# Attention and mixing with the last 64 rows, tokens and keys padded to 128

## Chip, cores and metric

One core of a Trainium2 chip. The metric is the device time of one execution in microseconds. Three runs of the kernel before took 1993.06, 1989.41 and 1990.96 us, a median of 1990.96.

## What is computed

Three stages follow each other on 8 batches (B) of 576 tokens (S) and 512 channels, all float32:

```
k_p, v_p = mean of k, v over groups of 8 keys          (576 -> 72 keys, 8 heads of 64)
attn = softmax(q k_p^T / 8) v_p                         per batch and head
x = heads side by side                                  (576 x 512 a batch)
u = x + (x^T U V)^T                                     U 576x32, V 32x576
x1 = u + relu(u w_ch1) w_ch2                            512 -> 2048 -> 512
u2 = x1 + real(fft2(x1));  un = layer norm of u2
out = u2 + relu(un w_ch1') w_ch2'                       512 -> 2048 -> 512
```

## The kernel before

The tokens of a batch are cut into five tiles, four of 128 and one of 64 (TT). The 8 heads x 72 pooled keys make 576 columns of scores, cut for the second attention matmul into five chunks, four of 128 and one of 64.

For each tile of a batch `tile_steps` (line 313) makes: scores, four float32 matmuls with q as weights against pooled keys laid out for pairs of heads (line 323), written to the two halves of PSUM; maximum (VectorE, line 334) and exp with sum (ScalarE, line 337) into the row buffer `s`; transposes of the five chunks on TensorE (lines 341 and 342) and copies of them to SBUF by ScalarE (lines 345 and 346); the product with v (line 353), five float32 matmuls with the transposed chunk as weights, the fifth of 64 keys; division by the sums (line 358); a split into a rounded part and a rest (line 366); and, one tile later, `hu_mm` (line 304), two float32r matmuls with U that sum over the tokens of all five tiles. `mix_split` and `mix_mm` (lines 396 and 403) then multiply by V tile by tile, add x, and store u. Pooling runs in `prep` (line 243): nine loads a batch through two buffers, each reduced by VectorE (lines 267 and 270). A float32 matmul appears in the records as two instructions, a float32r one as one. All matmuls but the transposes are on line 102, a helper.

The MLP is the bulk of the work: `st1` (line 645) sends 24 or 12 float32r matmuls of 256 columns a slot, `st2` (line 673) six of 512 columns a block and slot. For each of 18 blocks of 256 tokens and each phase there are 16 slots. Everything else is written as generators (lanes), and the main loop (line 818) takes one step of each lane a slot, between the first and second matmuls of the MLP. So the attention of batches 1 to 7 lies between the matmuls of the first MLP. Batch 0 is done before the loop, with three tiles in work at a time (`first`, line 372), next to the decoding of the weights from float64 words (`w_first`, line 129), whose last part is a subtraction on GpSimd (line 142). In batch 0 the second and third buffer sets (`alt` 1 and 2) are scratch tiles in the place of weights that have not come yet.

The planner of the tile framework orders the instructions of each engine by simulated times and priorities; from the second group of blocks on, ScalarE's order is that of the program text. Loads and stores go out on SP's queue.

Of the kernel before, what the change touches and what calls it, by code (L numbers as in the profile page):

```python
# [8 lines left out]
F32 = mybir.dt.float32  # L9
F32R = mybir.dt.float32r  # L10
I32 = mybir.dt.int32
ACTF = mybir.ActivationFunctionType
# [5 lines left out]
B, H, S, D = 8, 8, 576, 64  # L18
DM, DFF, RANK, POOL = 512, 2048, 32, 8
SP = S // POOL  # L20
NPAIR = H // 2
# [6 lines left out]
TT = [(0, 128), (128, 128), (256, 128), (384, 128), (512, 64)]  # L28
# [10 lines left out]
def kernel(  # L39
# [18 lines left out]
    nc = tc.nc  # L58
# [6 lines left out]
    ident = const.tile([128, 128], F32, name="ident")  # L65
# [6 lines left out]
    def scratch(i, w=1024, dt=F32):  # L72

        return wp.tile([128, w], dt, tag=f"w{i % 2}_{NF - 1 - i // 2}", name=f"scr{i}")

    xd = [[dram.tile([n, DM], F32, name=f"x{b}_{t}") for t, (_, n) in enumerate(TT)] for b in range(B)]
# [5 lines left out]
    def bank(tag):  # L82
        return ps_b.tile([128, 512], F32, tag=tag, name=tag)

    def mbank():
        if not state["free"]:
            state["n"] += 1
            return bank(("s0", "o0", "h0", "s1", "o1", "h1")[state["n"] % 6])
        return bank(state["m"])
# [4 lines left out]
    def add(eng, o, a, b):  # L94
        eng.tensor_tensor(out=o, in0=a, in1=b, op=ALU.add)

    def split(hi, lo, src, eng=None):
        nc.scalar.activation(out=hi, in_=src, func=ACTF.Copy)  # L98
        sub(eng or nc.vector, lo, src, hi.bitcast(F32))

    def mm(o, a, b, start, stop):
        nc.tensor.matmul(o, a, b, start=start, stop=stop, skip_group_check=True)  # L102
# [95 lines left out]
    class Attn:  # L198
        def __init__(self, c):
            p1 = self.p = c.enter_context(tc.tile_pool(name="at", bufs=1))  # L200
            self.k = p1.tile([128, NPAIR, 2 * SP], F32, name="k")
            self.v = p1.tile([128, 12, D], F32, name="v")
            self.mask = p1.tile([128, 12], F32, name="vmask")
            self.ust = p1.tile([128, 5, 4, RANK], F32R, name="ust")
            self.vst = p1.tile([128, S], F32R, name="vst")
            self.kp = {}
            self.hu = {}
            self.q = {}
            self.raw = {}
            self.mixing = False  # L210
            self.done = {}
            self.x0 = [None] * 5

        def setup(self):
            nc.vector.memset(self.k, 0.0)
            nc.gpsimd.dma_start(out=self.mask, in_=vmask)

        def tmp(self):
# [70 lines left out]
        def q_load(self, i):  # L289

            b, t = divmod(i, 5)
            if b == B:
                return
            r0, n = TT[t]
            q = self.p.tile([128, NPAIR, 128], F32, tag="q", name="q", bufs=3)
            nc.sync.dma_start(out=q[:, :, :n], in_=qT[b, :, :, r0:r0 + n].rearrange("a p s -> p a s"))
            self.q[b, t] = q

        def xtile(self, b):
# [2 lines left out]
            return self.p.tile([128, DM], F32, tag="xr", name="x", bufs=2)  # L302

        def hu_mm(self, b, t, xh, xl):
            n = TT[t][1]
            if t == 0:
                self.hu[b] = bank("hu")
            o = self.hu[b]
            w = self.ust[:n, t].rearrange("p g r -> p (g r)")
            mm(o, w, xh[:n], t == 0, False)  # L310
            mm(o, w, xl[:n], False, t == 4)

        def tile_steps(self, b, t, alt=0, before=None):
            p1 = self.p
            r0, n = TT[t]

            def banks():
                return [bank("soh"[alt] + i) for i in "01"]
            q = self.q.pop((b, t))
            sc = banks()  # L320
            for p in range(NPAIR):
                o = sc[p // 2][:n, (p % 2) * 144:(p % 2) * 144 + 144]
                mm(o, q[:, p, :n], self.k[:, p], p % 2 == 0, True)
            self.q_load(5 * b + t + 3)
            if before:
                before()
            sf = scratch(3 + alt) if alt else p1.tile([128, S], F32, tag="s", name="s")
            s = sf[:, 0:S].rearrange("p (h k) -> p h k", h=H)
            mx = p1.tile([128, H], F32, tag="mx", name="mx", bufs=2)
            sm = p1.tile([128, H], F32, tag="sm", name="sm", bufs=2)  # L330
            for i in range(2):
                h = slice(4 * i, 4 * i + 4)
                v = sc[i][:n, 0:288].rearrange("p (h k) -> p h k", h=4)
                nc.vector.tensor_reduce(out=mx[:n, h], in_=v, op=ALU.max, axis=AX.X, negate=True)  # L334
                for k in range(4):
                    a = 4 * i + k
                    nc.scalar.activation(out=s[:n, a], in_=v[:, k], func=ACTF.Exp, bias=mx[:n, a:a + 1], accum_out=sm[:n, a:a + 1])  # L337
            yield
            e0, e1 = banks()
            for c in range(4):  # L340
                nc.tensor.transpose(e0[:, c * 128:c * 128 + n], sf[:n, c * 128:c * 128 + 128], ident[:n, :n])  # L341
            nc.tensor.transpose(e1[:64, :n], sf[:n, 512:S], ident[:n, :n])
            e = scratch(4 + 2 * alt, 640) if alt else p1.tile([128, 640], F32, tag="e", name="e")
            e = e.rearrange("p (c k) -> p c k", c=5)
            nc.scalar.activation(out=e[:, 0:4, :n], in_=e0.rearrange("p (c k) -> p c k", c=4)[:, :, :n], func=ACTF.Copy)  # L345
            nc.scalar.activation(out=e[0:64, 4, :n], in_=e1[0:64, :n], func=ACTF.Copy)
            nc.vector.tensor_scalar(out=sm[:n], in0=sm[:n], scalar1=1e-9, scalar2=None, op0=ALU.add)
            nc.vector.reciprocal(out=sm[:n], in_=sm[:n])
            yield
            o = bank("soh"[alt] + "0")  # L350
            for c, (v0, h0, nh) in enumerate(VSLOT):
                k = min(128, H * SP - 128 * c)
                mm(o[:n, h0 * D:(h0 + nh) * D], e[:k, c, :n], self.v[:k, v0:v0 + nh].rearrange("p h d -> p (h d)"), c == 0, c == 4)
            if b == 0:
                xf = self.x0[t] = scratch(12 + t, 512)
            else:
                xf = self.xtile(b)
            nc.vector.tensor_tensor(out=xf[:n].rearrange("p (h d) -> p h d", h=H), in0=o[:n].rearrange("p (h d) -> p h d", h=H),
                                    in1=sm[:n].unsqueeze(2).to_broadcast([n, H, D]), op=ALU.mult)
            if alt:  # L360
                xx = scratch(9 + alt, dt=F32R)
                xh, xl = xx[:, 0:512], xx[:, 512:1024]
            else:
                xh = p1.tile([128, DM], F32R, tag="xh", name="xh")
                xl = p1.tile([128, DM], F32R, tag="xl", name="xl")
            split(xh[:n], xl[:n], xf[:n])
            if b:
                nc.sync.dma_start(out=xd[b][t], in_=xf[:n])
            self.done[t] = (xh, xl)
            yield  # L370

# [31 lines left out]
        def mix_mm(self, b, t, x):  # L403
            r0, n = TT[t]
            o = mbank()
            mm(o[:n], self.vst[:, r0:r0 + n], self.hst, True, True)
            add(nc.vector, x[:n], o[:n], x[:n])
            nc.sync.dma_start(out=ud[b * S + r0:b * S + r0 + n, :], in_=x[:n])
            if t == 4:
                self.mixing = False  # L410
# [347 lines left out]
    g = at.prep(0)  # L758
# [29 lines left out]
    for j in range(2):  # L788
        g = block_prep(0, j, at.x0[2 * j:])
# [198 lines left out]
```

## Time and profile before

| | |
|---|---|
| median of three runs | 1990.96 us |
| profiled execution: its own time | 1994.14 us |
| profiled execution: its span | 1992.4 us |
| TensorE matmul busy | 1925.2 us, 97% |
| TensorE weight load busy | 1712.2 us, 86% |
| VectorE busy | 837.7 us, 42% |
| ScalarE busy | 534.4 us, 27% |
| GpSimd busy | 213.7 us, 11% |
| mean granted TensorE clock | 0.986 |

Busy time is that in which at least one instruction of the engine is in work. Matmuls are pipelined: the next starts before the one before has ended, and their ends are modelled, so a matmul's row gives more than it takes of the engine. In the rows, PE is TensorE's matmul, PEld its weight load, DVE VectorE, ACT ScalarE, POOL GpSimd, and SPq the queue of SP. An entry such as 64*128 behind MATMUL gives the rows and the columns of the array that are in use; 64x64 behind it is the moving operand.

### The profile page before, as it was taken

Reading aid. Unit: us, or ns where it says so; the run is one execution under the profiler, and the core shown is the slowest. Engines: PE = TensorE matmul, PEld = TensorE weight load, DVE = VectorE, ACT = ScalarE, POOL = GpSimd, SP = SyncE. Lnnn points to the kernel's source line nnn. Section 1 sums busy time; section 2 is a strip of 40 time slices with the busy share of each in tenths; the row PEclk is TensorE's granted clock in tenths of the full one; section 3 lists DMA queues with packets and bytes.
Section 4 is the critical chain, followed back from the end, with each engine's and each line's share of the span. In section 5 each row is a group of like instructions: output and inputs, shape, how many; then the busy total and the mean of one; then the engine's idle time right before and its main releaser. Section 6 shows DMA issues by size and latency. Waiting matters only on the chain.

```text
span 1992.4 us, 31308 instructions
## 1 busy us (share of the span) xinstructions
PE 1925.2 (97%) x12220; PEld 1712.2 (86%) x12220; DVE 837.7 (42%) x1906; ACT 534.4 (27%) x1709; POOL 213.7 (11%) x323
## 2 busy tenths in 40 slices
PE   5689999999999999999999999999999999999999
PEld 3478888887888888999999899999999999999998
DVE  7984444444453443333334734444433222222221
ACT  6562333332333332122222422212111111111111
POOL 3530000000000000010112511211210000000000
PEclk8699999999999999999999999999999999999999
DMA  9434344435352423242234622322321111101110
GB/s 355 168 101 143 107 132 133 153 114 162 104 156 89 134 86 117 80 138 71 76 93 128 194 69 66 100 84 69 104 70 38 32 38 32 38 32 33 32 33 32
DMA packets 122740, 196.16 MB, mean 98 GB/s; under 512 B 17440, under 2 KB 42112, under 8 KB 122592
## 3 DMA queue, kind: packets, MB, share of 16 engines
q1 hardware_dynamic: 121664, 190.76, 30.5%
q0 software_dynamic: 928, 3.40, 0.5%
q8 instruction: 96, 1.57, 0.3%
q14 instruction: 52, 0.43, 0.1%
HBM read 139.72 MB, written 54.39 MB: 97 GB/s over the span
## 4 chain that ended last, share of the span: by engine, by line
PE 83%; DMA 7%; DVE 6%; issue 2%; POOL 1%; SPq 1%; ACT 0%; DVEq 0%; POOLq 0%; ACTq 0%
PE h L102 37%; PE o L102 36%; PE s L102 6%; DMA raw<-vr 1%; PE m L640 1%; PE hu L102 1%; DMA cv<-w1b 1%; POOL w L92 1%; DMA raw<-kT 1%; DVE scr L121 1%; DVE scr L122 1%; DVE vp L270 1%; DVE scr L116 1%; PE s L341 1%; DMA R<-x1d 1%
## 5 line engine op out<-in xcount | busy, mean ns | idle before, releaser
L102 PE MATMUL h<-uth,w 128*128 128x256 f32 x4608 | 931.0, 284 | 6.3 <-DVE hl L667 4.7
L102 PEld LDWEIGHTS h<-uth,w 128*128 128x128 f32 x4608 | 754.0, 190 | 36.4 <-DVE hl L667 10.0
L102 PE MATMUL o<-w,hh 128*128 128x512 f32 x2208 | 678.1, 398 | 3.1 <-ACT hh L666 3.0
L102 PE MATMUL h<-utl,w 128*128 128x256 f32 x2304 | 652.3, 283 | 0.0
L667 DVE SCALAR_TENSOR_TENSOR hl<-h,hh 128x256 fp32r<-128x256 f32 x560 | 234.2, 420 | 629.9 <-ACT hh L666 628.4
L666 ACT ACTIVATE hh<-h 128x256 fp32r<-128x256 f32 x560 | 214.9, 384 | 996.0 <-PE h L102 939.8
L102 PEld LDWEIGHTS h<-utl,w 128*128 128x128 f32 x2304 | 438.7, 190 | 21.1 <-issue 1.0
L102 PEld LDWEIGHTS o<-w,hh 128*128 128x128 f32 x2208 | 386.2, 189 | 62.0 <-ACT hh L666 4.8
L102 PE MATMUL o<-w,hl 128*128 128x512 f32 x1104 | 411.9, 395 | 0.6 <-DVE hl L667 0.6
L102 PEld LDWEIGHTS o<-w,hl 128*128 128x128 f32 x1104 | 198.6, 189 | 35.4 <-DVE hl L667 1.8
L337 ACT ACTIVATE s<-s,mx 128x72 f32<-128x72 f32 (+1 forms) x296 | 90.0, 326 | 61.6 <-DVE mx L334 61.3
L116 DVE TENSOR_SCALAR cv<-cv 128x256 int32<-128x256 int32 x64 | 18.9, 296 | 126.0 <-DMA cv<-w1b 70.1
L102 PE MATMUL s<-k,q 128*128 128x144 f32 (+1 forms) x296 | 53.4, 306 | 18.7 <-DMA scr<-vr 14.5
L92 DVE TENSOR_TENSOR utl<-m,uth 128x512 fp32r<-128x512 f32 x66 | 45.4, 687 | 55.8 <-ACT uth L98 55.4
L102 PEld LDWEIGHTS s<-v,e 128*128 128x128 f32 (+3 forms) x370 | 55.0, 183 | 15.4 <-issue 11.2
L102 PE MATMUL s<-v,e 128*128 128x192 f32 (+5 forms) x370 | 65.4, 314 | 0.9 <-ACT e L345 0.7
L631 POOL TENSOR_TENSOR rs<-mv,mhalf 128x1 f32<-128x1 f32 x36 | 20.9, 597 | 419.0 <-DVE mv L630 419.0
L102 PEld LDWEIGHTS s<-k,q 128*128 128x128 f32 (+1 forms) x296 | 42.3, 189 | 25.1 <-ACT k L277 14.5
L337 ACT ACTIVATION_READ_ACCUMULATOR s<-s,mx 128x1 f32 (+1 forms) x296 | 62.9, 213 | 0.0
L98 ACT ACTIVATE uth<-m 128x512 fp32r<-128x512 f32 x66 | 39.5, 598 | 75.1 <-PE m L640 75.1
L285 POOL TENSOR_TENSOR v<-vp,vmask 128x128 f32<-128x128 f32 x8 | 3.5, 435 | 506.4 <-PE s L102 495.8
L92 POOL TENSOR_TENSOR w<-scr,w 128x512 fp32r<-128x512 f32 x28 | 43.8, 1574 | 50.6 <-ACT w L98 40.5
(216 smaller groups left out, 1523.7 us busy)
## 6 DMA issues: line engine op xcount, KB each, us to landing
x<-x SPq DMA_DIRECT2D x56, 256.0 KB
ur<-ud SPq DMA_DIRECT2D x36, 256.0 KB
x1d<-ur SPq DMA_DIRECT2D x36, 256.0 KB
ul<-u2d SPq DMA_DIRECT2D x36, 256.0 KB
ur<-u2d SPq DMA_DIRECT2D x36, 256.0 KB
out<-ur SPq DMA_DIRECT2D x36, 256.0 KB
q<-qT SPq DMA_DIRECT2D x32, 256.0 KB
wraw<-w1a SPq DMA_DIRECT2D x16, 512.0 KB
```

The lines of the kernel that those rows point to most:

```text
L92: eng.tensor_tensor(out=o, in0=a, in1=b, op=ALU.subtract)
L98: nc.scalar.activation(out=hi, in_=src, func=ACTF.Copy)
L102: nc.tensor.matmul(o, a, b, start=start, stop=stop, skip_group_check=True)
L116: nc.vector.tensor_scalar(out=t, in0=lw, scalar1=29, scalar2=None, op0=ALU.logical_shift_right)
L121: nc.vector.scalar_tensor_tensor(out=t, in0=hw, scalar=-0x80000000, in1=t, op0=ALU.bitwise_and, op1=ALU.bitwise_or)
L122: nc.vector.scalar_tensor_tensor(out=t, in0=lw, scalar=3, in1=t, op0=ALU.logical_shift_left, op1=ALU.bitwise_or)
L270: nc.vector.tensor_reduce(out=vp[:n, i - 4, :], in_=t[:n, 0:512].rearrange("p (s e) -> p s e", e=POOL), op=ALU.add, axis=AX.X)
L337: nc.scalar.activation(out=s[:n, a], in_=v[:, k], func=ACTF.Exp, bias=mx[:n, a:a + 1], accum_out=sm[:n, a:a + 1])
L341: nc.tensor.transpose(e0[:, c * 128:c * 128 + n], sf[:n, c * 128:c * 128 + 128], ident[:n, :n])
L631: nc.gpsimd.tensor_tensor(out=rs[:, 0:1], in0=v, in1=mhalf, op=ALU.pow)
L666: nc.scalar.activation(out=hh, in_=p, func=ACTF.Relu)
L667: nc.vector.scalar_tensor_tensor(out=hl, in0=p, scalar=0.0, in1=hh.bitcast(F32), op0=ALU.max, op1=ALU.subtract)
```

## The change

The scores buffer becomes one tile of 640 columns that lives as long as the attention, with its last 64 columns zero, so that the fifth chunk of keys is 128 wide; the scratch buffers of batch 0 get the same by a memset for each tile. The upper half of v's fifth chunk is zero. q is padded on the host to 640 tokens, so that the fifth tile has 128 tokens, and V's buffer on the chip to 640 columns. U was padded on the host already. The stores still write 64 rows of the fifth tile.

```diff
             self.v = p1.tile([128, 12, D], F32, name="v")
+            self.s = p1.tile([128, 640], F32, name="s")
...
-            self.vst = p1.tile([128, S], F32R, name="vst")
+            self.vst = p1.tile([128, 640], F32R, name="vst")
...
         def setup(self):
             nc.vector.memset(self.k, 0.0)
+            nc.gpsimd.memset(self.v[64:128, 11], 0.0)
+            nc.gpsimd.memset(self.vst[:, S:640].bitcast(F32), 0.0)
+            nc.gpsimd.memset(self.s[:, S:640], 0.0)
...
-            nc.sync.dma_start(out=q[:, :, :n], in_=qT[b, :, :, r0:r0 + n].rearrange("a p s -> p a s"))
+            nc.sync.dma_start(out=q, in_=qT[b, :, :, 128 * t:128 * t + 128].rearrange("a p s -> p a s"))
...
         def hu_mm(self, b, t, xh, xl):
-            w = self.ust[:n, t].rearrange("p g r -> p (g r)")
-            mm(o, w, xh[:n], t == 0, False)
-            mm(o, w, xl[:n], False, t == 4)
+            w = self.ust[:, t].rearrange("p g r -> p (g r)")
+            mm(o, w, xh, t == 0, False)
+            mm(o, w, xl, False, t == 4)
...
         def tile_steps(self, b, t, alt=0, before=None):
-            r0, n = TT[t]
+            n = 128
...
-            sf = scratch(3 + alt) if alt else p1.tile([128, S], F32, tag="s", name="s")
+            sf = scratch(3 + alt) if alt else self.s
+            if alt:
+                nc.gpsimd.memset(sf[:, S:640], 0.0)
...
-            nc.tensor.transpose(e1[:64, :n], sf[:n, 512:S], ident[:n, :n])
+            nc.tensor.transpose(e1[:, :n], sf[:n, 512:640], ident[:n, :n])
...
-            nc.scalar.activation(out=e[0:64, 4, :n], in_=e1[0:64, :n], func=ACTF.Copy)
+            nc.scalar.activation(out=e[:, 4, :n], in_=e1[:, :n], func=ACTF.Copy)
...
-                k = min(128, H * SP - 128 * c)
-                mm(o[:n, h0 * D:(h0 + nh) * D], e[:k, c, :n], self.v[:k, v0:v0 + nh].rearrange("p h d -> p (h d)"), c == 0, c == 4)
+                mm(o[:n, h0 * D:(h0 + nh) * D], e[:, c, :n], self.v[:, v0:v0 + nh].rearrange("p h d -> p (h d)"), c == 0, c == 4)
...
-                nc.sync.dma_start(out=xd[b][t], in_=xf[:n])
+                nc.sync.dma_start(out=xd[b][t], in_=xf[:TT[t][1]])
...
         def mix_mm(self, b, t, x):
-            mm(o[:n], self.vst[:, r0:r0 + n], self.hst, True, True)
+            mm(o, self.vst[:, r0:r0 + 128], self.hst, True, True)
```

## Rows read from the trace of the kernel before

**Rows 1.** Three stretches: stretch, length, busy us of each engine (instructions), PEclk, DMA share, GB/s

```profile
0.00:130.00 130.00, 82.26 (x389) 63.63 (x389) 115.44 (x197) 75.83 (x245) 54.67 (x48) 0.79 0.64 224
130.00:760.00 630.00, 617.77 (x3861) 531.93 (x3860) 276.56 (x642) 215.42 (x861) 19.32 (x34) 1.00 0.41 125
760.00:1992.00 1232.00, 1225.14 (x7973) 1116.61 (x7971) 445.69 (x1068) 243.12 (x604) 139.71 (x241) 1.00 0.23 72
```

**Rows 2.** TensorE's timeline, full arrays: start us, busy us, engine, line, op, tiles

```profile
205.00 0.39 PE L102 MATMUL m<-w,hl 128*128 128x512 f32 x1
205.24 0.65 PE L102 MATMUL s<-k,q 128*128 128x144 f32 x4
205.63 1.62 PE L102 MATMUL o<-w,hw 128*128 128x512 f32 x6
...
208.56 0.60 PE L640 MATMUL s<-ident,ul 128*128 128x128 f32 x4
209.00 0.27 PE L341 MATMUL s<-ident,s 128*128 128x128 f32 x1
```

**Rows 3.** TensorE's timeline, the last keys of a 128-token tile

```profile
213.00 0.28 PE L102 MATMUL h<-uth,w 128*128 128x256 f32 x1
213.21 0.43 PE L102 MATMUL s<-v,e 64*128 64x64 f32 x2
213.57 0.76 PE L102 MATMUL s<-k,q 128*128 128x144 f32 x4
214.07 0.38 PE L102 MATMUL h<-uth,w 128*128 128x256 f32 x1
```

**Rows 4.** TensorE's timeline, scores of a fifth tile

```profile
355.25 0.28 PE L102 MATMUL h<-utl,w 128*128 128x256 f32 x1
355.37 0.28 PE L102 MATMUL h<-uth,w 128*128 128x256 f32 x1
355.58 0.70 PE L102 MATMUL s<-k,q 128*64 128x144 f32 x4
356.21 0.73 PE L102 MATMUL o<-w,hh 128*128 128x512 f32 x2
```

**Rows 5.** TensorE's timeline, before and after the transposes of a fifth tile

```profile
363.55 0.28 PE L102 MATMUL h<-uth,w 128*128 128x256 f32 x1
...
366.14 0.39 PE L102 MATMUL o<-w,hl 128*128 128x512 f32 x1
```

**Rows 6.** TensorE's timeline, the U matmuls of a fifth tile (two between)

```profile
280.64 0.28 PE L102 MATMUL h<-uth,w 128*128 128x256 f32 x1
280.85 0.50 PE L102 MATMUL hu<-xh,ust 64*128 64x512 f32 x1
...
281.73 0.28 PE L102 MATMUL h<-utl,w 128*128 128x256 f32 x1
```

**Rows 7.** TensorE's timeline, V's last columns

```profile
398.73 0.39 PE L102 MATMUL m<-hst,vst 128*64 128x512 f32 x1
398.96 0.40 PE L102 MATMUL o<-w,hl 128*128 128x512 f32 x1
```

**Rows 8.** Groups by form, weight loads of scores: busy us, mean ns | idle before

```profile
L102 PEld LDWEIGHTS s<-k,q 128*128 128x128 f32 x240 | 36.2, 201 | 22.9 <-ACT k L277 14.5 <-DVE x L358 3.5 <-DVE utl L92 2.0
L102 PEld LDWEIGHTS s<-k,q 128*64 128x64 f32 x56 | 6.1, 136 | 2.1 <-issue 0.4 <-ACT w L98 0.4
```

**Rows 9.** Groups by form, ScalarE's copy of four transposed chunks

```profile
L345 ACT ACTIVATE e<-s 128x512 f32<-128x512 f32 x30 | 17.9, 598 | 39.7 <-PE s L341 39.6
L345 ACT ACTIVATE e<-s 128x256 f32<-128x256 f32 x7 | 2.7, 384 | 20.9 <-PE s L341 20.9
```

**Rows 10.** One line's instructions, GpSimd's memset: duration ns min/median/max

```profile
L489 POOL MEMSET E<- x24: 98/98/140, 870.8 to 1431.7; 128x1 f32 x16, 99x1 f32 x8
```

**Rows 11.** Timeline of all engines: a reduction of v, a mixing matmul

```profile
299.32 0.69 DVE L270 TENSOR_REDUCE vp<-raw 128x64 f32<-128x512 f32 x1 [2.40 <-DMA raw<-vr]
...
301.27 0.50 PE L102 MATMUL m<-hst,vst 128*128 128x512 f32 x1 [0.98 <-DVE x L95]
```

More of the change, by code (lines that the diff above doesn't have):

```diff
@@ L304, in hu_mm @@
         def hu_mm(self, b, t, xh, xl):
-            n = TT[t][1]
             if t == 0:
@@ L308, in hu_mm @@
             o = self.hu[b]
-            w = self.ust[:n, t].rearrange("p g r -> p (g r)")
-            mm(o, w, xh[:n], t == 0, False)
-            mm(o, w, xl[:n], False, t == 4)
+            w = self.ust[:, t].rearrange("p g r -> p (g r)")
+            mm(o, w, xh, t == 0, False)
+            mm(o, w, xl, False, t == 4)
         def tile_steps(self, b, t, alt=0, before=None):
             p1 = self.p
-            r0, n = TT[t]
+            n = 128
             def banks():
@@ L966 @@
     arrays = {
-        "qT": con(q[:, horder][:, :, tok].transpose(0, 1, 3, 2).reshape(B, NPAIR, 128, S)),
+        "qT": con(np.pad(q[:, horder][:, :, tok].transpose(0, 1, 3, 2).reshape(B, NPAIR, 128, S), ((0, 0), (0, 0), (0, 0), (0, 64)))),
         "kT": con(k[:, horder].transpose(0, 1, 3, 2).reshape(B, NPAIR, 128, S)),
```

## The prediction

> **What bounds the kernel now.** I read the windows view first, in three stretches [rows 1]. From 130 us on TensorE sets the time: 617.8 of 630 us busy between 130 and 760 us, where the attention of batches 1 to 7 runs between the matmuls of the first MLP, and 1225.1 of 1232 us after that. The clock is 1.00 there, the 2.4 GHz level. Before 130 us VectorE is busy 115.4 of 130 us and TensorE only 82.3, at a mean clock of 0.79: saved TensorE time buys little there. Everything that the change touches runs before 760 us, so the question is what one matmul less, or one wait less, is worth between 130 and 760 us.
>
> Busy time can't show that, because matmuls are pipelined and overlap in the rows. So I went on to TensorE's timeline and read **starts**: the distance from one start to the next is what an instruction really takes of the engine. A float32 matmul stands there as two records. On full 128x128 arrays the distances are steady [rows 2]: a 512-column record 0.24 us (205.00 to 205.24), four records of float32 scores 0.39 us up to the next float32r matmul (205.24 to 205.63), a 128-column transpose 0.11 us (four from 208.56 to 209.00). A 256-column record takes 0.12 us (355.25 to 355.37) [rows 4]. A mix of types or of tiles alone costs nothing.
>
> Then the places where half of the array is used. In [rows 3] the last 64 keys of a tile, 64*128, follow a 256-column matmul: 0.21 us from 213.00 to 213.21 in place of 0.12, then 0.36 for the two, then 0.50 for the four full score records in place of 0.39. So the matmul before, the pair itself and what follows are all late: the array empties when its shape changes, on the way in and on the way out.
>
> **The change, part by part.** Each term is the stretch of starts as it stands, less the same records at the full distances.
>
> Last keys, tiles 0 to 3. 213.00 to 214.07 takes 1.07 us [rows 3]; full it would be 0.12 + 2 x 0.11 + 0.39 = 0.73. That is 0.34 us a tile. There are 28 such tiles in batches 1 to 7, two of which still lie before 130 us: 26 x 0.34 = 8.8 us.
>
> Fifth tile, scores. 355.37 to 356.21 takes 0.84 us [rows 4]; full 0.12 + 0.39 = 0.51. That is 0.33 us for each of two groups a batch: 14 x 0.33 = 4.6 us.
>
> Fifth tile, transposes. The planner lays the five among five 512-column matmuls in three groups; from 363.55 to 366.14 takes 2.59 us [rows 5], full 0.12 + 5 x 0.11 + 5 x 0.24 = 1.87. That is 0.72 us a batch: 7 x 0.72 = 5.0 us.
>
> Fifth tile, values. One group a batch, 128*64 and then 64*64. I price it like the last keys above: 7 x 0.34 = 2.4 us.
>
> Fifth tile, U. The pair from 280.64 to 281.73 takes 1.09 us [rows 6]; full 0.12 + 2 x 0.24 + 0.12 = 0.72, so 0.37 us. Where the planner puts the two apart, each changes the shape for itself and it is twice that. Between 7 x 0.37 = 2.6 and 5.2 I take 3.9 us.
>
> Two edits save nothing. V's last columns run 128*64 but in float32r, and 398.73 to 398.96 is 0.23 us, the distance of a full one [rows 7]: this shape is not a change of mode here, so padding V is worth 0. The transpose of the last 64 keys in tiles 0 to 3 (128*64 too) I count at 0 for the same reason.
>
> Together 24.7 us.
>
> What is added:
> - Full records that the trace lacks, float32 with 64 columns on 128 rows: I took 0.11 us, the 128-column transpose being the nearest. By columns alone it could be 0.055; the 144-column score record gives 0.12 as the upper end. For 70 records that is 3.9 us more gain to 0.7 us less.
> - The fifth tile loads 128 columns of weights in place of 64. The load's own row grows from 136 to 201 ns [rows 8], but the four score records of 128 columns go by in 0.39 us [rows 2] although each load lasts 0.2: loads run ahead under matmuls. I take 0.
>   The Trainium skill ("TensorE: Matmul & The Clock Gate", LDWEIGHTS) says that a load's time goes with its columns, not its rows; the trace agrees on the load's row and not on the distance between matmuls.
> - ScalarE's copy of the transposed fifth tile grows from 256 to 512 columns, 384 to 598 ns [rows 9], 0.21 us once a batch. The next step of that lane comes a step of the main matmuls later, which covers it; uncovered it is 7 x 0.21 = 1.5 us.
> - Six memsets on GpSimd, three of them in batch 0 ahead of the transposes of tiles 1, 2 and 4. The nearest row is 98 ns for 128x1 [rows 10]. Their queue is busy 54.7 of the first 130 us, so one can stand behind a weight split; those tiles lie where VectorE is the bound. I take 0, ends 0 and 1.5 us. The other three run once, before their tiles are used.
> - Eight loads of q, once a batch, carry 256 KB in place of 128: the DMA share is 0.41 [rows 1]. I take 0.
> - VectorE and ScalarE instructions on 128 partitions in place of 64 with the same columns: 0; the cover is the same as today.
>
> **What of it reaches the end.** TensorE takes its instructions in order, so each saving moves all that follows earlier, until it waits for something that does not move. TensorE idles 12.2 us between 130 and 760 us [rows 1]; such a wait stands at 301.27, where VectorE stood 2.40 us for a load of v and the mixing matmul came 0.98 us late [rows 11]. Waits of that kind grow when TensorE is early. I give back a fifth of the idle time, 2.5 us; ends 0 and the whole 12.2. Net 22.2 us, against the profiled execution's own 1994.1 us (span 1992.4): 1971.9. That execution is 3.2 us above the median of the runs, 1990.96, so the forecast is **1968.8 us**.
>
> **Rivals.**
> - Half is given back. The order on TensorE and VectorE is planned anew with other costs, and the idle time of this stretch doubles: 24.7 - 12.2 = 12.5 us, 1978.5. For it: the waits on loads above. Against: only 2% of the stretch is idle now.
> - The weight loads count. Loads of 64 columns become 128 for 20 records of the fifth tile (8 scores, 10 values, one transpose, one of V) and for one transpose in each of the other four. If such a load can't run ahead, each costs 201 - 136 = 65 ns [rows 8]: 7 x 24 x 0.065 = 10.9 us, gain 22.2 - 10.9 = 11.3, 1979.7. Against it stand the distances in [rows 2].
>   [...]
> - More. The 64-column records go at 0.055 us, and the start gains some microseconds because batch 0 changes shape too, at the lower clock: a gain of 28 to 31 us, about 1961.
> - Nothing moves. The lateness comes from the type or the lane's waits and not from the half-used array, so that padding leaves it: 1991. Against it: [rows 2] has the same types with no lateness.
> - Slower. VectorE waits at the head of its queue for the loads of k and v, nine a batch and 63 in all; an earlier TensorE meets these loads before they land, and each stands before an addition that the mixing needs. Priced at the 0.98 us of [rows 11], 63 such come to 62 us; from 26 on they eat the gain. With 40 the time would be 1991 + 39 - 25 = 2005. Against it: VectorE is busy 277 of 630 us only, and today's waits come to 12 us in all.
>
> **How the numbers follow.** Forecast (gain 14 to 28) 0.62, half given back 0.11, weight loads 0.06, more 0.05: faster 0.84. Nothing moves 0.07. Slower 0.09. About 0.2%, 4 us, is what a measurement of this kernel can tell from no change. The range reaches from the "more" case (1961) to a gain of only 5 us (1986): the slower case and nothing moves stay out, 0.16.
>
> **What would show it.** In the profile after, no matmul of 64 rows should be left; the distances around the last keys should be 0.12, 0.11 and 0.39; the stretch from 130 to 760 us should be some 22 us shorter with TensorE still above 97% busy, and the first 130 us and everything after the attention as long as before. I am wrong if the distances shrink and the idle time grows by as much (give-back), if the distances of the fifth tile's score records rise above 0.122 (loads), or if the first stretch changes by more than 3 us.

## The result and the profile after

The changed kernel takes 1974.01 us (median of 5 runs, 1972.53 to 1974.65) where the kernel before takes 1990.89 (5 runs, 1989.41 to 1993.06): a ratio of 0.9915, 95% interval 0.99 to 0.9929, 16.9 us less. The forecast was 1968.8 us, with a range of 1961 to 1986: right in sign and cause, 5.2 us too hopeful in size. The profiled execution of the changed kernel took 1974.01 us itself, with a span of 1972.2; between the two profiled executions lie 20.1 us.

The same three stretches as in [rows 1], the windows view of the changed kernel (length, then busy us of TensorE, its weight loads, VectorE, ScalarE and GpSimd, granted clock, DMA share, GB/s):

```profile
0.00:130.00 130.00, 80.35 (x403) 65.67 (x404) 117.20 (x199) 77.94 (x248) 51.44 (x55) 0.83 0.66 226
130.00:760.00 630.00, 612.93 (x3973) 551.51 (x3972) 283.99 (x660) 220.71 (x867) 17.93 (x34) 1.00 0.42 131
760.00:1972.00 1212.00, 1204.67 (x7849) 1098.47 (x7847) 437.34 (x1048) 239.61 (x594) 140.12 (x241) 1.00 0.22 70
```

Between 130 and 760 us TensorE now puts 3973 matmuls through where it put 3861, and idles 17.1 us where it idled 12.2. In the first 130 us VectorE is as busy as before, and TensorE is 14 matmuls further on.

TensorE's timeline at the same places. The last keys of a tile, to set beside [rows 3]:

```profile
213.69 0.28 PE L102 MATMUL h<-uth,w 128*128 128x256 f32 x1
213.81 0.33 PE L102 MATMUL s<-v,e 128*128 128x64 f32 x2
213.98 0.71 PE L102 MATMUL s<-k,q 128*128 128x144 f32 x4
214.43 0.38 PE L102 MATMUL h<-uth,w 128*128 128x256 f32 x1
```

213.69 to 214.43 is 0.74 us; it was 1.07, and the prediction had 0.73. The two records of 64 columns on 128 rows, which the trace before did not have, take 0.17 us, 0.085 each, and the four scores behind them 0.45 in place of 0.39; the stretch is as long as with the 0.11 us each that was taken. The transposes of a fifth tile, beside [rows 5], with the same five transposes and five 512-column matmuls in between:

```profile
356.67 0.28 PE L102 MATMUL h<-uth,w 128*128 128x256 f32 x1
...
358.50 0.40 PE L102 MATMUL o<-w,hl 128*128 128x512 f32 x1
```

1.83 us in place of 2.59; the prediction had 1.87. And U's pair, beside [rows 6]:

```profile
277.42 0.28 PE L102 MATMUL h<-uth,w 128*128 128x256 f32 x1
277.54 0.40 PE L102 MATMUL hu<-xh,ust 128*128 128x512 f32 x1
277.77 0.40 PE L102 MATMUL hu<-xl,ust 128*128 128x512 f32 x1
278.01 0.62 PE L102 MATMUL o<-w,hh 128*128 128x512 f32 x2
```

0.12, 0.23 and 0.24 us: full distances. So each stretch shown here came out at the full length that the sum had taken for it. I then took the whole trace from 130 us to the end of the attention, and added up, for each group on half an array, its stretch of starts less the full distances (512 columns 0.232 us, 256 0.120, float32 scores 0.122 a record, float32 products of 192 columns 0.163, the others 0.109). Before, 74 groups had 24.7 us of lateness. After, none is left.

Of these 24.7 us, 20.1 show between the two profiled executions and 16.9 between the medians. The experiments ask what became of the rest, and whether it is the shape that costs.

### The profile page after: what moved, and what is told of

It is laid out like the page before. It is cut to its first block, busy times and chain, and to the rows that moved or that the text cites. A ratio compares the mean times of both kernels' runs of the same rounds, so it can differ in the third digit from the quotient of the medians.

```text
span 1972.2 us, 31326 instructions
## 1 busy us (share of the span) xinstructions
PE 1898.0 (96%) x12220; PEld 1715.7 (87%) x12220; DVE 838.5 (43%) x1906; ACT 538.3 (27%) x1709; POOL 209.5 (11%) x329
## 4 chain that ended last, share of the span: by engine, by line
PE 82%; DMA 8%; DVE 6%; issue 1%; ACT 1%; SPq 1%; POOL 0%; DVEq 0%; ACTq 0%
PE h L102 38%; PE o L102 35%; PE s L102 6%; DMA raw<-vr 2%; DMA raw<-kT 1%; PE m L644 1%; PE hu L102 1%; DMA ud<-x 1%; DMA cv<-w1b 1%; DVE scr L122 1%; DMA q<-qT 1%; DMA ul<-ud 1%; DVE scr L121 1%; DMA wraw<-w2a 1%; DVE scr L116 1%
## 5 line engine op out<-in xcount | busy, mean ns | idle before, releaser
L342 ACT ACTIVATE s<-s,mx 128x72 f32<-128x72 f32 x296 | 90.3, 329 | 61.7 <-DVE mx L339 61.5
L102 PE MATMUL s<-k,q 128*128 128x144 f32 x296 | 50.6, 295 | 16.0 <-ACT k L281 12.9
L342 ACT ACTIVATION_READ_ACCUMULATOR s<-s,mx 128x1 f32 x296 | 63.7, 215 | 0.0
L102 PEld LDWEIGHTS s<-v,e 128*128 128x128 f32 x370 | 59.3, 194 | 4.0 <-issue 0.7
L102 PEld LDWEIGHTS s<-k,q 128*128 128x128 f32 x296 | 42.6, 193 | 19.9 <-ACT k L281 12.9
L102 PE MATMUL s<-v,e 128*128 128x192 f32 (+2 forms) x370 | 58.6, 305 | 0.7 <-ACT e L350 0.5
L95 DVE TENSOR_TENSOR ur<-o,ur 128x512 f32<-128x512 f32 x70 | 46.5, 685 | 4.6 <-PE o L102 3.4
```

## The experiments

Each run is compared with runs of the kernel before on the same chip. Those had medians of 1992.3, 1992.3 and 1991.9 us for the three sets of runs below, so from set to set the ratios are compared, not the times.

### The parts alone

`e1_keys`: the kernel before, with the padding of the last 64 keys and nothing else.

```diff
+            self.s = p1.tile([128, 640], F32, name="s")
...
+            nc.gpsimd.memset(self.v[64:128, 11], 0.0)
+            nc.gpsimd.memset(self.s[:, S:640], 0.0)
...
-            sf = scratch(3 + alt) if alt else p1.tile([128, S], F32, tag="s", name="s")
+            sf = scratch(3 + alt) if alt else self.s
+            if alt:
+                nc.gpsimd.memset(sf[:, S:640], 0.0)
...
-            nc.tensor.transpose(e1[:64, :n], sf[:n, 512:S], ident[:n, :n])
+            nc.tensor.transpose(e1[:, :n], sf[:n, 512:640], ident[:n, :n])
...
-            nc.scalar.activation(out=e[0:64, 4, :n], in_=e1[0:64, :n], func=ACTF.Copy)
+            nc.scalar.activation(out=e[:, 4, :n], in_=e1[:, :n], func=ACTF.Copy)
...
-                k = min(128, H * SP - 128 * c)
-                mm(o[:n, h0 * D:(h0 + nh) * D], e[:k, c, :n], self.v[:k, v0:v0 + nh].rearrange("p h d -> p (h d)"), c == 0, c == 4)
+                mm(o[:n, h0 * D:(h0 + nh) * D], e[:, c, :n], self.v[:, v0:v0 + nh].rearrange("p h d -> p (h d)"), c == 0, c == 4)
```

> The padding of the last 64 keys alone, put into the kernel before; the fifth tile and V stay as they were. Theory (the array empties at each change of shape): the two distances around the last keys of tiles 0 to 3 fall by 0.34 us each, 26 of them where TensorE is the bound, and for the fifth tile's last keys (64*64 becomes 128*64) a little more: 9 us less on TensorE, of which waits on loads take back 1 to 3, so 6 to 8 us faster than before. Rival (the lateness belongs to the lane's waits or to the type): below 2 us. Rival (the given-back time is all in the fifth tile's part): 9 us faster.

`e2_fifth`: the reverse, the changed kernel with the memsets, transpose, copy and product of the last 64 keys as they were before (shown: the product).

```diff
...
-                mm(o[:n, h0 * D:(h0 + nh) * D], e[:, c, :n], self.v[:, v0:v0 + nh].rearrange("p h d -> p (h d)"), c == 0, c == 4)
+                k = min(128, H * SP - 128 * c)
+                mm(o[:n, h0 * D:(h0 + nh) * D], e[:k, c, :n], self.v[:k, v0:v0 + nh].rearrange("p h d -> p (h d)"), c == 0, c == 4)
```

> The fifth tile widened to 128 tokens and V padded, without the padding of the last 64 keys. Theory: the fifth tile's scores, transposes, values and U lose their changes of shape, but the last keys keep one in every tile, the fifth's among them: 4.6 + 5.0 + 3.9 + about 0.3 = 13.8 us less on TensorE, of which 2 to 5 are given back: 9 to 12 us faster than before. With the last keys alone the two gains should add up to the 16.9 us of the whole change within 3. Rival (a wider weight load costs its 65 ns): 3 us or less faster, and distances above 0.122 us between the score records of the fifth tile.

Measured: `e2_fifth` 1983.31 us, ratio 0.9959 (0.9947 to 0.9972), 9.0 us faster, in the range. `e1_keys` 1990.75, ratio 0.999 (0.9981 to 0.9998): 1.5 us faster, where 6 to 8 were expected and "below 2" was the rival's. The two gains add to 10.5, not to 16.9.

But the lateness did go. Added up in the same way, 16.2 us of the 24.7 are left in the trace of `e1_keys`, so 8.5 went; 10.4 are left in that of `e2_fifth`, so 14.3 went. What took most of the 8.5 us back stands in the timeline of `e1_keys`, all engines (in brackets the idle time before, and what ended it; `hw` is the rounding rest of the first MLP's hidden values, which TensorE multiplies next):

```profile
170.06 0.33 SPq L187 DMA_DIRECT2D wd<-cv  x1
170.48 0.38 SPq L179 DMA_DIRECT2D cv<-w1b  x1
173.62 0.29 DVE L116 TENSOR_SCALAR cv<-cv 128x256 int32<-128x256 int32 x1 [3.59 <-DMA cv<-w1b]
173.95 0.42 DVE L671 SCALAR_TENSOR_TENSOR hw<-h,hw 128x256 fp32r<-128x256 f32 x1
...
174.43 0.73 PE L102 MATMUL o<-w,hw 128*128 128x512 f32 x2 [3.67 <-DVE hw L671]
```

The weights of the second MLP are decoded meanwhile, one load at a time. The load goes out at 170.48, after the store of the part before; VectorE reaches the part at the head of its queue and stands 3.59 us; the rest `hw` is next in that queue; TensorE stands 3.67 us. Another 1.27 us go at 164.31 in the same way, behind a load of v. In the kernel before TensorE's waits are 0.3 us in all between 150 and 200 us. In the changed kernel the same place costs 1.83 us, this time behind a load of v:

```profile
167.47 1.07 PE L102 MATMUL o<-w,hw 128*128 128x512 f32 x4
...
169.30 0.69 DVE L274 TENSOR_REDUCE vp<-raw 128x64 f32<-128x512 f32 x1 [1.88 <-DMA raw<-vr]
169.90 0.41 DVE L671 SCALAR_TENSOR_TENSOR hw<-h,hw 128x256 fp32r<-128x256 f32 x1
...
170.37 0.73 PE L102 MATMUL o<-w,hw 128*128 128x512 f32 x2 [1.83 <-DVE hw L671]
```

The kernel before has the same reduction, with the same wait, in front of the same `hw`:

```profile
168.70 2.00 PE L102 MATMUL o<-w,hw 128*128 128x512 f32 x6
168.89 0.69 DVE L270 TENSOR_REDUCE vp<-raw 128x64 f32<-128x512 f32 x1 [1.88 <-DMA raw<-vr]
169.49 0.41 DVE L667 SCALAR_TENSOR_TENSOR hw<-h,hw 128x256 fp32r<-128x256 f32 x1
```

VectorE waits 1.88 us in both, but TensorE starts these matmuls at 168.70 before and at 167.47 after, and stands only after: here an earlier TensorE meets a load that did not move. In `e1_keys` this is not so clear, since the planner put a part of the weights, and not the reduction of v, ahead of this `hw`. VectorE's order differs between these kernels in places up to about 190 us, and how much of the loss comes from the order and how much from the earlier TensorE is not separated.

### V's padding, and 96 rows

`e3_noV` leaves V's last columns at 64.

```diff
-            mm(o, self.vst[:, r0:r0 + 128], self.hst, True, True)
+            mm(o[:n], self.vst[:, r0:r0 + n], self.hst, True, True)
```

> The changed kernel, with V's last columns left at 64 (128*64, float32r). Theory: this shape does not empty the array, so the time is that of the changed kernel within 1.5 us, 1972.5 to 1975.5. Rival (every 64-column load is a change of shape): 7 x 0.3 = 2 us slower, and distances after V's last columns 0.1 us longer.

1975.74 us, ratio 0.9916 (0.9903 to 0.9929): the ratio of the changed kernel, 0.9915. By the time alone the rival's 2 us can't be told from this, but its trace shows the 64-column products of V that follow a steady stream at 0.23 to 0.24 us to the next start, full distances. The padding of V brings nothing.

`e4_rows96` multiplies the last keys on 96 rows, neither 64 nor 128.

```diff
+                k = 96 if c == 4 else 128
-                mm(o[:n, h0 * D:(h0 + nh) * D], e[:, c, :n], self.v[:, v0:v0 + nh].rearrange("p h d -> p (h d)"), c == 0, c == 4)
+                mm(o[:n, h0 * D:(h0 + nh) * D], e[:k, c, :n], self.v[:k, v0:v0 + nh].rearrange("p h d -> p (h d)"), c == 0, c == 4)
```

> The changed kernel, with the last keys' product on 96 rows (64 keys and 32 rows of zeros) in place of 128. Theory (the array is cut in parts, and a shape that fits into a part makes it empty): 96 rows do not fit into half of the array, so no lateness, and the time is that of the changed kernel within 1.5 us; distances 0.16, 0.11. Rival (any height below 128 makes the array empty): 9 us slower than the changed kernel, all of the last keys' part. Rival (the lateness goes with the share of rows left out): half of it, 4 us slower.

1974.95 us, ratio 0.9913 (0.9901 to 0.9926). Its TensorE timeline at the last keys:

```profile
214.69 0.28 PE L102 MATMUL h<-uth,w 128*128 128x256 f32 x1
214.81 0.33 PE L102 MATMUL s<-v,e 96*128 96x64 f32 x2
214.98 0.71 PE L102 MATMUL s<-k,q 128*128 128x144 f32 x4
215.43 0.38 PE L102 MATMUL h<-uth,w 128*128 128x256 f32 x1
```

0.74 us from 214.69 to 215.43, as on 128 rows. The lateness does not go with the share of the rows that is left out; it comes with 64 rows and not with 96. The Trainium skill ("TensorEngine Tiling (Array Packing)", Tiling Modes) says that a change of tiling mode drains TensorE; the trace agrees for 64*128, and for 128*64 in float32 only (below). In these traces the drain is 0.09 us on the way in and some 0.2 to 0.25 from there until the distances are regular again.

### What the loads hold

Now the loads. `e5_raw3` gives the loads of k and v a third buffer and one more load ahead.

```diff
-            return self.p.tile([128, S], F32, tag="raw", name="raw", bufs=2)
+            return self.p.tile([128, S], F32, tag="raw", name="raw", bufs=3)
...
-            ahead = 9 if b == 0 else 2
+            ahead = 9 if b == 0 else 3
```

> The changed kernel with three buffers in place of two for the loads of k and v (raw), three loads ahead. Theory A (what the saving lost between 150 and 215 us is VectorE standing at the head of its queue for loads of k and v): the waits of VectorE for raw loads, 19 and 8 us in the changed kernel between 130 and 760 us, fall by half or more, TensorE's waits between 150 and 215 us fall from 4.8 us to below 2, and the kernel is 2 to 4 us faster than the changed one: 1970 to 1972. Theory B (it stands there for the loads of the second MLP's weights, cv): within 1.5 us of the changed kernel.

`e8_ahead` loads the second MLP's weights a step ahead.

```diff
-            return self.p.tile([128, 512], F32, tag="cv", name="cv", bufs=2)
+            return self.p.tile([128, 512], F32, tag="cv", name="cv", bufs=3)
...
+        load(0)
         for i in range(n):
-            load(i)
             t = tmp()[:, 0:256].bitcast(I32)
             yield
             high(raws[i], 256, t)
+            if i + 1 < n:
+                load(i + 1)
             yield
```

> The changed kernel with the second MLP's weights loaded one step ahead through three buffers (cv) in place of two. Theory B: VectorE's wait for cv loads, 101 us between 130 and 760 us, falls to below 30; TensorE's waits between 150 and 215 us fall from 4.8 us to below 2, and the kernel is 2 to 6 us faster than the changed one: 1968 to 1972. Theory A: within 1.5 us of the changed kernel. Rival C (it is the planner's order and no one wait): the waits move elsewhere, the time stays.

Each alone brings nothing, where 2 to 4 and 2 to 6 us were hoped for. `e5_raw3` 1974.17 us, ratio 0.991 (0.9897 to 0.9924); `e8_ahead` 1975.8, ratio 0.992 (0.9907 to 0.9934): the time of the changed kernel. With the third raw buffer VectorE's waits for v fall from 18.7 to 8.7 us, but at this place VectorE still stands 1.00 us for weights and then 2.12 us for v, and TensorE 3.13 us. With the weights ahead VectorE hardly waits for them any more, and the groups view (130 to 760 us, the changed kernel first, `e8_ahead` below it) shows it:

```profile
L116 DVE TENSOR_SCALAR cv<-cv 128x256 int32<-128x256 int32 x54 | 15.8, 293 | 101.6 <-DMA cv<-w1b 64.5 <-DMA cv<-w2b 36.9
```

```profile
L116 DVE TENSOR_SCALAR cv<-cv 128x256 int32<-128x256 int32 x54 | 15.5, 287 | 6.1 <-DMA cv<-w2b 2.7 <-issue 1.6 <-DMA cv<-w1b 1.1
```

95 us less of waiting on VectorE, and nothing at the end: most of it was idle time that nobody needed, and the loads of k and v still stand in the queue (2.41 us for k at 158.87). TensorE's waits between 150 and 215 us fall from 4.8 to 3.6 us only. This is what rival C expected. So I put the two together, into the changed kernel (`e9_both`) and into the kernel before (`e10_before_both`), the edits being those of `e5_raw3` and `e8_ahead`.

```diff
+            return self.p.tile([128, S], F32, tag="raw", name="raw", bufs=3)
...
+            ahead = 9 if b == 0 else 3
...
+            return self.p.tile([128, 512], F32, tag="cv", name="cv", bufs=3)
...
+                load(i + 1)
```

> The changed kernel with both: three buffers for the loads of k and v, and the second MLP's weights loaded a step ahead. If the give-back is made of both waits the gains add up: TensorE's idle time between 130 and 760 us falls from 17 us to below 10, the time to 1964 to 1969. Rival C: no change beyond 2 us.

> The kernel before with both of these. If the loads take the saving back only because TensorE comes earlier, the kernel before gains less from them than the changed kernel does: 0 to 3 us, and the changed kernel with both stands 20 to 25 us ahead of this one, near the 24.7 us that the distances gave. If the loads hold both alike, both gain the same and the difference stays at 17.

`e9_both` 1972.53 us, ratio 0.9901 (0.9886 to 0.9917): the lowest median here, though not clear of the changed kernel. TensorE's waits between 150 and 215 us are down from 4.8 to 1.8 us, but its idle time from 130 to 760 us is 14.2 us, not below 10, and 1964 to 1969 was missed: by the time alone rival C holds. `e10_before_both` 1994.01 us, ratio 1.0011 (1.0002 to 1.002): no gain, if anything 2 us lost. The distance between the two is 21.5 us, in the 20 to 25 that was expected, against 16.9 without the loads ahead. The 4.6 us more are not clear of noise: by the intervals of the ratios the change is worth 14 to 20 us without the loads ahead and, estimated from the intervals of `e9_both` and `e10_before_both`, some 18 to 25 with them.

The part that had brought almost nothing is the sharper test. `e11_keys_both` is `e1_keys`, `e12_fifth_both` is `e2_fifth`, each with the loads ahead.

```diff
+            return self.p.tile([128, S], F32, tag="raw", name="raw", bufs=3)
...
+            ahead = 9 if b == 0 else 3
...
+            return self.p.tile([128, 512], F32, tag="cv", name="cv", bufs=3)
...
+                load(i + 1)
```

> The padding of the last 64 keys alone, now with the loads ahead as in e10 (three buffers for k and v, the second MLP's weights a step ahead). In the trace of the keys alone the distances had given 8.5 us and the time only 1.5. Theory (an earlier TensorE meets loads that do not move): with the loads ahead most of the 8.5 reaches the end, 6 to 9 us below e10's 1994.0: 1985 to 1988. Rival (the padding itself costs something that no distance shows): 1 to 3 us below e10, 1991 to 1993.

> The widened fifth tile and V alone, with the loads ahead. The distances gave 14.3 us, the time 9.0. Theory: 11 to 15 us below e10's 1994.0: 1979 to 1983, and the gains of keys and fifth tile add up to the 21.5 us between e10 and e9 within 3. Rival: 9 us again, 1985.

`e11_keys_both` 1986.54 us, ratio 0.9973 (0.9962 to 0.9983): 7.5 us below `e10_before_both`, where the same padding had been worth 1.5. `e12_fifth_both` 1982.5, ratio 0.9953 (0.9938 to 0.9967): 11.5 us below. Together 19.0, within 3 of 21.5. The rival, a hidden cost of the padding itself, is out. Some 3 of the 7.5 us are not the padding's, though: in `e10_before_both` TensorE stands 2.96 us at 166.45, behind two reductions of v that waited for their loads, and the three other kernels with the loads ahead have no such stall. Against the kernel before as it was, `e11_keys_both` is 5.4 us faster.

Where in time this happens can be read from one matmul stream that all kernels share. These are the starts (us) of three of the 4608 matmuls of the first kind in [rows 3] (`h<-uth`), the 129th, the 257th and the 1409th, the last of which comes after the attention:

```
                   129th    257th   1409th
before            155.10   209.85   767.94
after             154.28   210.53   747.65
e1_keys           156.85   215.68   766.38
e2_fifth          156.30   212.37   757.50
e10_before_both   155.95   210.95   766.80
e9_both           154.77   207.31   744.35
e11_keys_both     154.95   207.34   757.43
e12_fifth_both    155.11   207.70   754.39
```

Between the 129th and the 257th matmul the kernel before takes 54.75 us; `e1_keys` takes 58.83, `e2_fifth` 56.07, the changed kernel 56.25, though each has less to do. `e1_keys` and `e2_fifth` are also 1.8 and 1.2 us later at the 129th. The loss is made before the 257th, in the first batch after the start, once: from 130 us to the 257th matmul TensorE waits 1.0 us before and 5.1 in the changed kernel, from there to the 1409th 11.3 and 12.0. After the 257th, `e1_keys` gains 7.4 us on the kernel before, `e2_fifth` 13.0 and the changed kernel 21.0, which do add up. With the loads ahead the three take 52.4 to 52.6 us from the 129th to the 257th, `e10_before_both` 55.00.

At the 1409th matmul the change is worth 20.29 us without the loads ahead (767.94 less 747.65) and 22.45 with them (766.80 less 744.35), 2.2 us more and not 4.6. What comes behind it is the same work in all four: 1224.5 us before and 1224.6 after, 1223.5 in `e10_before_both` and 1226.6 in `e9_both`. This scatter between single executions is as large as the difference in question.

### U alone, and a form that V does not have

`e13_U64` puts U's matmuls of the fifth tile back on 64 rows; the rows left out are zeros.

```diff
-            w = self.ust[:, t].rearrange("p g r -> p (g r)")
-            mm(o, w, xh, t == 0, False)
-            mm(o, w, xl, False, t == 4)
+            n = TT[t][1]
+            w = self.ust[:n, t].rearrange("p g r -> p (g r)")
+            mm(o, w, xh[:n], t == 0, False)
+            mm(o, w, xl[:n], False, t == 4)
```

> The changed kernel with U's two matmuls of the fifth tile back on 64 rows (the rows left out are zeros). Theory (each change of shape empties the array and costs 0.37 to 0.4 us): 11 such places in batches 1 to 7, 4.3 us more on TensorE, 2 to 4.3 us slower than the changed kernel: 1976 to 1978.3. Rival (TensorE is no longer the bound here, loads are): within 1 us of the changed kernel.

1979.77 us, ratio 0.9935 (0.9918 to 0.9951) against 0.9915: about 4 us slower than the changed kernel by the ratios, 5.8 by the medians, above the range that was expected; the intervals of the two ratios just overlap. Its trace has 4.4 us of lateness in the 11 places, where the prediction had priced U at 3.9, and reaches the 1409th matmul at 754.56 us, 6.9 behind the changed kernel. A lateness of TensorE still reaches the end here, so TensorE is still the bound.

`e7_v_f32` is the kernel before, with V's last columns multiplied in float32.

```diff
+            if t == 4:
+                mm(o[:n], self.vst[:, r0:r0 + n].bitcast(F32), self.hst.bitcast(F32), True, True)
+            else:
+                mm(o[:n], self.vst[:, r0:r0 + n], self.hst, True, True)
```

> The kernel before with V's last 64 columns (128*64) multiplied in float32 in place of float32r: two records of 512 columns instead of one, some 0.2 to 0.7 us more each of 8 times. Theory (only the float32 form of 128*64 cuts the array in two): the distance into the pair grows by 0.09 and the one behind it by 0.2 us above the records' own, as the scores of the fifth tile show. Rival (no 128*64 of 512 columns empties the array, whatever its type): distances into it and out of it as on a full array.

It ran once; the time, 2001.39 us, is not used. TensorE's timeline:

```profile
506.04 1.07 PE L102 MATMUL o<-w,hh 128*128 128x512 f32 x4
507.04 1.07 PE L102 MATMUL m<-hst,vst 128*64 128x512 f32 x2
508.04 0.39 PE L102 MATMUL h<-uth,w 128*128 128x256 f32 x1
508.26 0.28 PE L102 MATMUL h<-utl,w 128*128 128x256 f32 x1
```

The four matmuls before the pair take 1.00 us in place of 4 x 0.23 = 0.92, and the one behind it 0.22 in place of 0.12: the array empties, though the way out costs 0.10 us and not the 0.2 that was expected. In [rows 7], the same shape in float32r, it doesn't.

## Why the prediction was right, and where its size was off

**What bounds.** TensorE from 130 us on: right. `e13_U64` gives 4.4 us of lateness back to TensorE and the time rises by at least about that. The parts that the change doesn't touch kept their length: the 129th matmul starts 0.8 us earlier, and what follows the attention takes 1224.5 us before and 1224.6 after.

**The terms of the sum.** 24.7 us of lateness was priced, and the whole trace counts 24.7; that the sums agree to the tenth is luck, since U was priced at 3.9 and has 4.4. The keys with the fifth tile's share went at 8.5 us, the rest of the fifth tile and U at 14.3, and 22.8 of 24.7 add up from the two alone (a group that loses one of its two neighbouring changes of shape keeps the other). Full 64-column records at 0.11 us (as a stretch), V at 0 and the weight loads at 0 held. The rival of the weight loads is out: float32 scores on full arrays go by at 0.122 us a record in the changed kernel too, fifth tiles included. So is "nothing moves".

**What of it reaches the end.** This is the step that failed, in size: "I give back a fifth of the idle time, 2.5 us". TensorE's idle time in the stretch rose by 4.9 us, from 12.2 to 17.1, and 4.6 of the 24.7 us are missing between the two profiled executions. The two go together: 24.7 less 4.9 is 19.8, and 20.3 us reach the 1409th matmul. The mechanism was the one that was named, VectorE standing for a load with something behind it that TensorE needs; but the place was wrong. I had looked at mixing additions behind the loads of k and v all through the attention. The runs showed it in the first batch after the start, mostly before the first MLP's `hw`, and behind the weights' loads as well as behind v's. Giving room to either alone changed nothing. Giving room to both took these waits of TensorE away (4.8 to 1.8 us), and the keys alone were then worth 5.4 to 7.5 us in place of 1.5; for the whole change the gain, 16.9 to 21.5 us by the medians, is not clear of noise. How much of the loss is the planner's other order, and not the loads, stays open.

**The offset.** The other 3.2 us are the distance of the one profiled execution of before to its median, which I carried over in full to the forecast. The changed kernel's profiled execution stood on its median. In the other runs with several executions this distance lies between 2.8 us below and 2.1 above. A single execution's distance to the median is scatter, not a part of the kernel.

**Half given back, slower.** The first came a good part of the way (17 of 24.7 reach the median), and for the keys alone 1.5 of 8.5 us reached the end. The slower case did not come: its stalls were priced at 0.98 us each and as many as 26 were needed; the profile has a handful, of up to 1.8 us.

## What to carry to other kernels

Read the cost of a matmul from start to start, and look for groups of starts that are late where the array's shape changes: a matmul on 64 of 128 rows between full ones cost 0.34 us, and zeros in the other 64 rows cost TensorE nothing. Padding is worth it for a lone small matmul in a dense stream; then look at what the stream meets earlier than before, since two waits for loads at the head of a queue took back 4.9 of a part's 8.5 us. Two parts that bring 10 us apart may bring 17 together, so a part that measures as nothing is not yet shown to be worth nothing.

## What the runs showed of the hardware

- 64*128 empties the array in float32 (the last keys) and in float32r (U); 96*128 does not.
- 128*64 empties it in float32 (scores, and V in `e7_v_f32`: 0.08 and 0.10 us), and not in float32r (V, 0.23 us to the next start). The float32 transpose on 128*64 (the last keys of a 128-token tile) cost nothing either: the changed kernel's transposes on 128*128 have the same distances. The Trainium skill ("TensorEngine Tiling (Array Packing)", Restrictions and Gotchas) lists column tiling and transposes of float32 as exclusive; the trace fits that, though no run shows that this is the reason. The float32r case stood in the trace of before already.
